# Attention and a gated feed-forward on one core: the weights' 64-bit words moved by four bytes in SBUF, and the output products' place in the order

## The chip, the cores and the metric

The kernel runs on one core of a Trainium2 chip. The metric is the device time of one execution, in microseconds. The engines are PE (TensorE, matrix products), DVE (VectorE), ACT (ScalarE), POOL (GpSimd) and SP (SyncE, which here issues every transfer). They run side by side, each its own instructions in the order in which the program has them; between engines they wait for semaphores.

## The reference

Attention over a window of 64 positions, 8 batches of 576 positions, 8 heads of 64, and behind it a feed-forward over 4,608 tokens from 512 to 2,048 and back to 512, with a piecewise gate:

```python
scores = np.where((rel >= 0) & (rel < window), scale * (q @ k.T), -1e9)   # rel = query position - key position
attn = softmax(scores) @ v
...
h = x @ w_in                                  # x: attention's output, 4608 x 512
g = np.where(h >= 1, h, np.where(h <= -1, 0.0, (h + 1) ** 2 / 4))
out = (g @ w_out).astype(np.float32)
```

q, k and v are float32; w_in and w_out are float64, and the kernel takes them as 64-bit words.

## The kernel before

**Tiles and steps.** The tokens are cut into twelve tiles (TILES): four of 256, six of 512, two of 256. Each tile runs the feed-forward in 16 steps f, one for each 128 of the 2,048 hidden channels. A step has two products on PE: the input product (`ffn_in`, L498), 12 matmuls into a PSUM bank `ps_h`, and the output product (`ffn_out`, L544), three matmuls for each 128 tokens, which add to the banks `acc`. Between them lies a chain over four engines: `ffn_relu` (L506, ACT), `ffn_square` (L512 on ACT, L514 on DVE), `ffn_gate` (L520, DVE, which also frees `ps_h`), `ffn_high` (L527, ACT, rounds the gate's result to `gh`) and `ffn_low` (L534, POOL, the rest `gl`). Each of `ps_h`, `a`, `gh` and `gl` has two buffers. The products take every operand as a high and a low part, so that three matmuls do the work of one exact one.

**Attention** goes in 36 blocks s of 128 tokens, ahead of the tile that needs them: scores on PE (L333), mask and maximum on DVE (L344, L348), exponentials on ACT (L355), inverse and normalization (L362, L363 and L367, DVE, now and then POOL), the transposition (L377, twelve instructions for each half of the heads on DVE, in two runs of six; in the first tiles on PE, L383, with a copy), the product with v (L397), and the result as a high part `xh` (a cast, L200 on ACT or L202 on DVE) and a low part `xl` (L413, DVE).

**Weights.** Each step needs a group of 64-bit words from w_in and w_out, 512 or 1,024 words a partition. They are loaded once (`w_load`, L218), in twenty transfers, into tiles of 16-bit numbers, `raw`. A 64-bit word is four such numbers, the lowest first. `w_rest` (L251, ACT) reads the two middle ones as one 32-bit integer (fraction) into `u`; `w_sign` (L228, ACT) reads the top one (sign and exponent) as bfloat16 and writes it into the front of the same tile; two limits (L232) and a shift (L244) on DVE bring the exponent to float32's place; `w_join` (L255, DVE) adds it to `u`; `w_high` (L202 or L200) casts `u` to the high part and `w_low` (L267, DVE) subtracts that from `u`. High and low part, `wts`, take the place of the raw words in SBUF. `u` has two buffers, so the third group's `w_rest` waits for the first one's `w_low`. The first four steps have two groups of 512 words each, the others one of 1,024.

[...] 

**The order** is the planner's (`Plan.run`). Each task has a key, and among the tasks that can start at about the same time on an engine (within PATIENCE; 0 on PE) the one with the lowest key is next. It reckons with costs in ns that are written in the code, and only the order comes out of it. An input product's key is `f * n / 384` past its tile's start, so in a 512 tile a step is 4/3 of a unit, in a 256 tile 2/3; the first two tiles run interleaved, 4/3 a step. The output product has the key of its input product plus `O_LAG`:

```python
x_out = add(
    key + O_LAG, dict(PE=3 * n / P * 232), lambda e, f=f: ffn_out(t, f),
    [xl, w_ready[f, 1]] + ([x_out] if f else []), ...
```

In the program as built, the twenty tiles of weights lie one behind the other at the end of SBUF, and each begins at a multiple of 32 bytes.

Of the kernel before, what the change touches and what calls it, by code (L numbers as in the profile page):

```python
# [12 lines left out]
U32 = mybir.dt.uint32  # L13
U16 = mybir.dt.uint16
# [6 lines left out]
P = 128  # L21
# [25 lines left out]
A_STEP = 4  # L47
A_SPAN = 8
A_LEAD = 5
O_LAG = 2.7  # L50
DMA_LAG = 2300
BEGIN = dict(PE=1500, ACT=2300, DVE=2500, SP=750)
PERIOD = 10240 / 3
# [11 lines left out]
class Plan:  # L65
# [9 lines left out]
    def add(self, key, cost, do, after=(), takes=(), gives=(), lag=0):  # L75
        self.work.append((key, cost, do, set(after), takes, gives, lag))
        return len(self.work) - 1
# [70 lines left out]
def banded_attention_then_ffn(ctx: ExitStack, tc: tile.TileContext, q, k, v, w, masks, out, dims):  # L148
    nc = tc.nc
# [30 lines left out]
    wpool = ctx.enter_context(tc.tile_pool(name="wpool", bufs=1))  # L180
# [25 lines left out]

    ws, wts, zs, us = {}, {}, {}, {}

    lowest, highest = 896 << 4, (1151 << 4) - 1

    def w_load(g):
        f, units = g
        m = len(units) * DM
        ws[g] = t = wpool.tile([P, 4 * m + 4], U16, name="raw", tag=f"w{f}_{units[0]}")
        src = w[f, :, units[0]:units[-1] + 1].bitcast(U16)
        nc.sync.dma_start(out=t[:, 1:4 * m + 1], in_=src.rearrange("p u n -> p (u n)"))  # L218

    def w_sign(g):  # L220

        m = len(g[1]) * DM
        t = ws[g].bitcast(BF16)
        zs[g] = z = t[:, :m]
        top = t[:, 4:4 * m + 4].rearrange("p (n h) -> p n h", h=4)[:, :, 0]
        nc.scalar.activation(z, top, AF.Prelu, scale=2.0 ** -48, alpha=2.0 ** -32)  # L228

    def w_limit(g, dt, lo, hi):  # L230
# [15 lines left out]
    def w_rest(g):  # L246

        m = len(g[1]) * DM
        us[g] = u = ffn.tile([P, 2 * DM], U32, name="u", bufs=BUFS["u"])[:, :m]
        rest = ws[g][:, 2:4 * m + 2].bitcast(U32).rearrange("p (n h) -> p n h", h=2)[:, :, 0]  # L250
        nc.scalar.activation(u, rest, AF.Copy, scale=2.0 ** -13)  # L251

    def w_join(g):
# [17 lines left out]
    def add_weights(f, units):  # L271
        g = f, units
        m = len(units) * DM
        act, dve1, dve2, dve4 = 93 + .833 * m, 68 + 1.0417 * m, 68 + .5208 * m, 68 + .2604 * m
        key = f * W_STEP - (W_FIRST[f] if f < len(W_FIRST) else W_LEAD) + .5 * units[0]
        x = add(W0_KEY + W0_STEP * (f + .5 * units[0]), dict(SP=W_LOAD * len(units)), lambda e: w_load(g), lag=DMA_LAG)
        xr = add(key - W_LATE, dict(ACT=act), lambda e: w_rest(g), [x], takes=["u"])
        x = add(key, dict(ACT=act), lambda e: w_sign(g), [xr])
        x = add(key, dict(DVE=dve4), lambda e: w_limit_signed(g), [x])
        x = add(key - W_LATE, dict(DVE=dve4), lambda e: w_limit_unsigned(g), [x])  # L280
        x = add(key - 2 * W_LATE, dict(DVE=dve4), lambda e: w_shift(g), [x])
        x = add(key - 3 * W_LATE, dict(DVE=dve1), lambda e: w_join(g), [x])
        x = add(key - 4 * W_LATE, dict(ACT=act, DVE=dve2), lambda e: w_high(g, e), [x])
        x = add(key - 5 * W_LATE, dict(DVE=dve1), lambda e: w_low(g), [x], gives=[("u", xr)])
        for u in units:
            w_ready[f, u] = x
# [250 lines left out]
    def ffn_out(t, f):  # L537
        _, gh, gl = gs.pop((t, f))
        if f == 0:
            acc[t] = [bank("acc") for _ in range(TILES[t] // P)]  # L540
        for i in range(TILES[t] // P):
            sub = slice(i * P, (i + 1) * P)
            for j, (g, part) in enumerate(((gh, 0), (gh, 1), (gl, 0))):
                nc.tensor.matmul(  # L544
                    acc[t][i], lhsT=g[:, sub], rhs=wts[f, 1][:, part], start=(f == 0 and j == 0),
                    stop=(f == NF - 1 and j == 2),
                )
# [16 lines left out]
    def add_ffn(t):  # L564
        n = TILES[t]
        x_out = None
        for f in range(NF):
# [14 lines left out]
            x_out = add(  # L582
                key + O_LAG, dict(PE=3 * n / P * 232), lambda e, f=f: ffn_out(t, f),
                [xl, w_ready[f, 1]] + ([x_out] if f else []), takes=["acc"] * (n // P) if f == 0 else [],
# [83 lines left out]
```

## Time and profile before

| | before |
|---|---|
| time, median of three runs | 944.24 us (942.72 to 944.29) |
| the profiled execution, its own time | 944.14 us |
| its span, first to last instruction | 942.4 us |
| PE busy | 916.6 us (97%) |
| DVE busy | 609.6 us (65%) |
| ACT busy | 462.7 us (49%) |
| POOL busy | 215.9 us (23%) |
| mean granted clock of PE | 0.994 |
| read from HBM, written | 59.44 MB, 9.44 MB |

The span is shorter than the execution's time by 1.7 us, which lie before its first and behind its last instruction. Busy time is a mean over stages that differ: the page has the span in 40 slices of 23.6 us, and there DVE is at nine tenths or more in the second to fifth, while PE is at nine tenths or more nearly throughout from the third on. The transfer engines are at eight tenths or more in the first two slices, at seven in the third, and at one or two tenths for most of the rest. A line that begins with a number is a timeline's (start in us, length in us, engine, line, operation, tiles written and read, count; in brackets how long the engine had been idle and what it waited for). In groups the columns behind the count are busy us and mean ns.

### The profile page before, as it was taken

The page shows a single profiled execution, that of the slowest core. Times are in us where ns is not written, and L with a number is a line of the kernel's source. Part 1 is how long each engine was busy: PE and PEld are TensorE (multiplying, and loading weights), DVE is VectorE, ACT ScalarE, POOL GpSimd, SP SyncE. Part 2 cuts the span into 40 slices and gives each one's busy share as a digit, 9 for nine tenths or more (in the row PEclk, how much of TensorE's full clock was granted, in tenths as well). Part 3 has the DMA queues.
Part 4 walks back from the last instruction along what each step waited for, and adds up shares of the span by engine and source line. Part 5 has one row for each costly group of instructions (what it writes and reads, how often), then busy time and mean ns, then how long its engine had stood idle before and what let it go on. Part 6 is the DMA issues. An engine that isn't in the chain of part 4 may idle for free.

```text
span 942.4 us, 16930 instructions
## 1 busy us (share of the span) xinstructions
PE 916.6 (97%) x6408; PEld 753.2 (80%) x6408; DVE 609.6 (65%) x1457; ACT 462.7 (49%) x1247; POOL 215.9 (23%) x204
## 2 busy tenths in 40 slices
PE   6798899999999999999999999999999999999998
PEld 5677788888887787777877777778777878888897
DVE  5999999897926755577466836683667561348511
ACT  5776766455534435444444434453445343436443
POOL 0132322222222212122212212122221222222222
PEclk8999999999999999999999999999999999999999
DMA  8971022222110212111211121211112020111000
GB/s 304 411 298 29 29 74 97 64 91 72 51 46 29 71 54 73 51 51 61 86 51 51 51 88 34 72 56 56 62 40 86 28 73 1 51 45 35 1 23 23
DMA packets 29025, 69.96 MB, mean 74 GB/s; under 512 B 3216, under 2 KB 3344, under 8 KB 27408
## 3 DMA queue, kind: packets, MB, share of 16 engines
q1 hardware_dynamic: 28944, 68.89, 21.4%
q8 instruction: 50, 0.82, 0.4%
q14 instruction: 31, 0.25, 0.1%
HBM read 59.44 MB, written 9.44 MB: 73 GB/s over the span
## 4 chain that ended last, share of the span: by engine, by line
PE 87%; DVE 7%; issue 3%; ACT 1%; POOL 1%; DMA 1%; SPq 0%; DVEq 0%; POOLq 0%; ACTq 0%
PE ps_h L498 40%; PE acc L544 40%; PE ps_a L397 4%; PE ps_a L333 3%; DVE u L255 2%; DVE raw L232 1%; DVE a L520 1%; DVE wts L202 1%; POOL gl L534 1%; DMA kt<-in_k 1%; DVE sm L367 1%; DVE raw L244 0%; DVE xl L413 0%; PE acc L397 0%; DVE wts L267 0%
## 5 line engine op out<-in xcount | busy, mean ns | idle before, releaser
L498 PE MATMUL ps_h<-xh,wts 128*128 128x256 f32 (+1 forms) x1536 | 408.8, 341 | 12.0 <-DVE a L520 8.9
L534 POOL TENSOR_TENSOR gl<-a,gh 128x256 fp32r<-128x256 f32 (+1 forms) x192 | 209.0, 1090 | 681.8 <-ACT gh L527 673.1
L544 PE MATMUL acc<-wts,gh 128*128 128x512 f32 x1152 | 364.9, 398 | 0.0
L498 PEld LDWEIGHTS ps_h<-xh,wts 128*128 128x128 f32 x1536 | 267.3, 188 | 57.0 <-DVE a L520 14.1
L498 PE MATMUL ps_h<-xl,wts 128*128 128x256 f32 (+1 forms) x768 | 259.3, 338 | 0.3 <-DVE xl L413 0.3
L544 PEld LDWEIGHTS acc<-wts,gh 128*128 128x128 f32 x1152 | 210.6, 188 | 46.4 <-issue 2.1
L520 DVE SCALAR_TENSOR_TENSOR a<-a,ps_h 128x256 f32<-128x256 f32 (+1 forms) x192 | 105.2, 553 | 215.3 <-ACT a L512 188.0
L544 PE MATMUL acc<-wts,gl 128*128 128x512 f32 x576 | 227.8, 395 | 0.1
L377 DVE STREAM_TRANSPOSE ptd<-sm 32x128 f32<-32x128 f32 x720 | 218.0, 303 | 12.4 <-POOL sm L367 0.9
L506 ACT ACTIVATE a<-ps_h 128x256 f32<-128x256 f32 (+1 forms) x192 | 93.6, 488 | 229.6 <-PE ps_h L498 219.4
L527 ACT CAST gh<-a 128x256 fp32r<-128x256 f32 (+1 forms) x192 | 97.5, 510 | 144.2 <-PE acc L544 120.0
L498 PEld LDWEIGHTS ps_h<-xl,wts 128*128 128x128 f32 x768 | 144.6, 188 | 18.4 <-DVE xl L413 0.5
L544 PEld LDWEIGHTS acc<-wts,gl 128*128 128x128 f32 x576 | 108.4, 188 | 26.8 <-POOL gl L534 1.1
L355 ACT ACTIVATE sm<-sm,nm 128x128 f32<-128x128 f32 x256 | 99.5, 390 | 52.9 <-DVE nm L348 52.9
L512 ACT ACTIVATE a<-a 128x512 f32<-128x512 f32 (+1 forms) x189 | 99.6, 527 | 5.9
L344 DVE SCALAR_TENSOR_TENSOR sm<-ps_a,msk 128x512 f32<-128x512 f32 x64 | 43.8, 684 | 13.2 <-PE ps_a L333 12.9
L413 DVE TENSOR_TENSOR xl<-ps_a,xh 128x512 fp32r<-128x512 f32 x34 | 23.5, 690 | 41.7 <-ACT xh L200 41.2
L367 DVE TENSOR_TENSOR sm<-sm,den 128x512 f32<-128x512 f32 x66 | 48.8, 739 | 2.3
L355 ACT ACTIVATION_READ_ACCUMULATOR sm<-sm,nm 128x1 f32 x256 | 47.9, 187 | 0.0
L348 DVE TENSOR_REDUCE nm<-sm 128x4 f32<-128x512 f32 x64 | 43.9, 686 | 2.1
L397 PEld LDWEIGHTS ps_a<-ptd,vt 128*64 128x64 f32 x1088 | 34.6, 138 | 12.7 <-PE acc L544 6.6
L333 PEld LDWEIGHTS ps_a<-kt,qt 64*64 64x64 f32 x1088 | 29.5, 132 | 13.3 <-issue 8.6
(54 smaller groups left out, 356.2 us busy)
## 6 DMA issues: line engine op xcount, KB each, us to landing
vt<-in_v SPq DMA_DIRECT2D x72, 256.0 KB, 2.9
kt<-in_k SPq DMA_DIRECT2D x36, 384.0 KB, 3.9
raw<-in_w SPq DMA_DIRECT2D x12, 1024.0 KB, 13.2
qt<-in_q SPq DMA_DIRECT2D x36, 256.0 KB, 2.7
out<-o SPq DMA_DIRECT2D x36, 256.0 KB, 2.0
raw<-in_w SPq DMA_DIRECT2D x8, 512.0 KB, 7.1
msk<-in_masks SPq DMA_DIRECT2D x1, 192.0 KB, 2.5
```

Source lines behind the costliest of these rows:

```text
L333: nc.tensor.matmul(banks[h][half[i], p, :], lhsT=qt[half[h], p, i * QB:(i + 1) * QB], rhs=kt[half[h], p, i * QB:i * QB + WIN], start=not m ...
L355: nc.scalar.activation(sm[:, p, :], (ps if masked else sm)[:, p, :], AF.Exp, bias=nm[:, p:p + 1], scale=scale if masked else 1.0, accum_ou ...
L367: engine[eng].tensor_tensor(out=sm, in0=sm, in1=den.unsqueeze(2).broadcast_to([P, NP, WIN]), op=ALU.mult)
L377: nc.vector.transpose(pt[c * SQ:(c + 1) * SQ, :, r], sm[r, :, c * SQ:(c + 1) * SQ])
L397: nc.tensor.matmul(ps[half[h], p, n], lhsT=vt[i][:, c:c + D], rhs=pt[h][:, p, n], start=True, stop=True)
L498: nc.tensor.matmul(ps[:, :n], lhsT=wts[f, 0][:, part, c * P:(c + 1) * P], rhs=x[:, c, :n], start=(c == 0 and j == 0), stop=(c == NP - 1 an ...
L506: nc.scalar.activation(gs[t, f][0][:, :n], phs[t, f][:, :n], AF.Relu, bias=0.5, scale=0.5)
L512: nc.scalar.activation(a[:, :n], a[:, :n], AF.Square)
L520: nc.vector.scalar_tensor_tensor(out=a[:, :n], in0=a[:, :n], scalar=1.0, in1=ps[:, :n], op0=ALU.min, op1=ALU.max)
L527: nc.scalar.copy(gh[:, :n], gs[t, f][0][:, :n])
L534: nc.gpsimd.tensor_tensor(out=gl[:, :n], in0=a[:, :n], in1=gh[:, :n].bitcast(F32), op=ALU.subtract)
L544: nc.tensor.matmul(acc[t][i], lhsT=g[:, sub], rhs=wts[f, 1][:, part], start=(f == 0 and j == 0), stop=(f == NF - 1 and j == 2),)
```

## The change

Two things. The load now drops the first 16-bit number of each partition's row and puts the rest at the tile's very start, so the middle numbers of a word begin at byte 0 and the top one at byte 4; the tile has no spare numbers, and a group takes 4,096 or 8,192 bytes a partition. (The dropped number is the lowest one of a row's first word, which nothing reads, as with the lowest ones of all other words.) And `O_LAG` goes from 2.7 to 2.5.

```diff
-O_LAG = 2.7
+O_LAG = 2.5
...
-        ws[g] = t = wpool.tile([P, 4 * m + 4], U16, name="raw", tag=f"w{f}_{units[0]}")
+        ws[g] = t = wpool.tile([P, 4 * m], U16, name="raw", tag=f"w{f}_{units[0]}")
         src = w[f, :, units[0]:units[-1] + 1].bitcast(U16)
-        nc.sync.dma_start(out=t[:, 1:4 * m + 1], in_=src.rearrange("p u n -> p (u n)"))
+        nc.sync.dma_start(out=t[:, :4 * m - 1], in_=src.rearrange("p u n -> p (u n)")[:, 1:])
...
-        top = t[:, 4:4 * m + 4].rearrange("p (n h) -> p n h", h=4)[:, :, 0]
+        top = t.rearrange("p (n h) -> p n h", h=4)[:, :, 2]
...
-        rest = ws[g][:, 2:4 * m + 2].bitcast(U32).rearrange("p (n h) -> p n h", h=2)[:, :, 0]
+        rest = ws[g].bitcast(U32).rearrange("p (n h) -> p n h", h=2)[:, :, 0]
```

A blank line was added too, so in the changed kernel every line behind L206 has a number higher by one (L544 is L545).

The layout alone changes no engine's order. O_LAG does. In a 512 tile, 2.7 lies just behind the key of the input product two steps on (2 x 4/3 = 2.67), 2.5 just ahead of it. The same holds for the first two tiles; in the other 256 tiles (2/3 a step) it is the input product four steps on. The order is the same up to about the eighth of the output products, some 53 us into the span; three places behind that follow.

PE in tile 6, where the input product of step 5 ends (`wts_816` is step 5's weights of the input side and of the output side, `wts_757` step 4's, `wts_699` step 3's; the numbers of the tiles in the other names don't matter). Before:

```order
L498 MATMUL ps_h_5217<-xl_4381,wts_816 128x512
L498 MATMUL ps_h_5217<-xh_4380,wts_816 128x512
L544 MATMUL acc_5117<-wts_699,gh_5188 128x512 x2
L544 MATMUL acc_5117<-wts_699,gl_5190 128x512
L544 MATMUL acc_5118<-wts_699,gh_5188 128x512 x2
```

and now:

```order
L499 MATMUL ps_h_5226<-xl_4408,wts_816 128x512
L499 MATMUL ps_h_5226<-xh_4407,wts_816 128x512
L545 MATMUL acc_5069<-wts_757,gh_5239 128x512 x2
L545 MATMUL acc_5069<-wts_757,gl_5241 128x512
L545 MATMUL acc_5070<-wts_757,gh_5239 128x512 x2
```

The output product behind step 5's input product was step 3's and is now step 4's.

ACT in the stage that prepares the weights, at about 60 us, from the relu and square of tile 1, step 3, to step 6's `w_sign` (L228; `raw_485` is step 6's group). L527 is the cast to `gh` of step 3, its first row tile 0, its second tile 1. Before:

```order
L506 ACTIVATE a_759<-ps_h_730 128x256
L512 ACTIVATE a_759<-a_759 128x256
L251 ACTIVATE u_770<-raw_485 128x1024
L527 CAST gh_789<-a_745 128x256
L527 CAST gh_792<-a_759 128x256
L228 ACTIVATE raw_485<-raw_485 128x1024
```

and now:

```order
L507 ACTIVATE a_766<-ps_h_744 128x256
L513 ACTIVATE a_766<-a_766 128x256
L528 CAST gh_771<-a_738 128x256
L528 CAST gh_791<-a_766 128x256
L252 ACTIVATE u_794<-raw_485 128x1024
L507 ACTIVATE a_813<-ps_h_775 128x256
L513 ACTIVATE a_813<-a_813 128x256
L229 ACTIVATE raw_485<-raw_485 128x1024
```

Both casts to `gh` now stand ahead of step 6's `w_rest`, and the relu and square of tile 0, step 4, ahead of its `w_sign`.

DVE from the last but one group's shift (L244) to the last group's limits (L232). Before:

```order
L244 TENSOR_SCALAR raw_826<-raw_826 128x1024
L255 TENSOR_TENSOR u_1266<-u_1266,raw_826 128x1024
L202 CAST wts_1546<-u_1266 128x2x512
L267 TENSOR_TENSOR wts_1546<-u_1266,wts_1546 128x2x512
L520 SCALAR_TENSOR_TENSOR a_1529<-a_1529,ps_h_1446 128x256
L232 TENSOR_SCALAR raw_864<-raw_864 128x1024
L413 TENSOR_TENSOR xl_1510<-ps_a_1550,xh_1509 128x4x128
```

and now:

```order
L245 TENSOR_SCALAR raw_825<-raw_825 128x1024
L256 TENSOR_TENSOR u_1270<-u_1270,raw_825 128x1024
L202 CAST wts_1565<-u_1270 128x2x512
L268 TENSOR_TENSOR wts_1565<-u_1270,wts_1565 128x2x512
L363 TENSOR_SCALAR den_1327<-den_1327 128x4
L364 RECIPROCAL den_1327<-den_1327 128x4
L368 TENSOR_TENSOR sm_1325<-sm_1325,den_1327 128x512
L521 SCALAR_TENSOR_TENSOR a_1511<-a_1511,ps_h_1457 128x256
L521 SCALAR_TENSOR_TENSOR a_1578<-a_1578,ps_h_1552 128x256
L233 TENSOR_SCALAR raw_863<-raw_863 128x1024 x2
```

An inverse and a normalization of block 5 now stand between the two, two gates stand together ahead of the last group's limits, and the xl subtraction is behind the last split.

## The prediction

> **What bounds the kernel now.** I began with the page: a span of 942.4 us and PE busy for 916.6 us of it, so some 26 us are to be had from waiting and the rest only from a faster pace of PE. Then I cut the span into stretches, to see where those 26 us lie.
>
> ```profile
> 0.00:53.00 53.00, 39.63 (x406) 31.62 (x407) 41.22 (x98) 36.28 (x112) 5.65 (x12) 0.90 0.96 365
> 53.00:137.30 84.30, 76.34 (x600) 64.69 (x598) 81.67 (x122) 58.10 (x129) 25.29 (x24) 1.00 0.24 85
> 137.30:938.20 800.90, 800.64 (x5405) 656.86 (x5404) 485.98 (x1239) 368.32 (x1008) 184.92 (x169) 1.00 0.17 54
> 938.20:942.40 4.20, 0.00 (x0) 0.00 (x0) 0.69 (x1) 0.00 (x0) 0.00 (x0) 0.92 0.34 127
> ```
>
> A row has the stretch and its length, then the busy time (and instructions) of PE, PEld, DVE, ACT and POOL, the granted clock, the DMA share and GB/s. Read the length against PE busy. Up to 53.0 us (filling) PE idles 13.4 us, from there to 137.3 us 8.0 us, then 0.3 us in 800.9, and 4.2 us at the end for the last store. So there are two machines. Until 137.3 us DVE sets the pace (81.7 of 84.3 us busy, and what the table doesn't count is the few tens of ns between instructions); afterwards it is PE alone. What hands over from one to the other stands in the timelines of DVE and PE:
>
> ```profile
> 133.96 1.37 DVE L255 TENSOR_TENSOR u<-u,raw 128x1024 uint16<-128x1024 uint16 x1
> 135.36 0.69 DVE L202 CAST wts<-u 128x1024 fp32r<-128x1024 f32 x1
> 136.09 1.23 DVE L267 TENSOR_TENSOR wts<-u,wts 128x1024 fp32r<-128x1024 f32 x1
> 137.23 0.41 DVE L520 SCALAR_TENSOR_TENSOR a<-a,ps_h 128x256 f32<-128x256 f32 x1
> ```
> ```profile
> 137.70 0.38 PE L498 MATMUL ps_h<-xh,wts 128*128 128x256 f32 x1 [0.26 <-DVE a L520]
> ```
>
> The last group of weights is split at 136.09, the gate of step 14 follows on DVE, and the product of tile 0, step 15 starts at once. From there PE never waits. **The time is therefore when DVE is through with that group and that gate, plus the PE work still to be done.**
>
> **The change part by part.** It has two: where the weights lie, and O_LAG, which only sets the order.
>
> *The layout.* No instruction is added or removed on PE, DVE, ACT or POOL; twenty loads carry 2 bytes less in each row. Could the old places have cost something? For the loads, set two stretches side by side, the first mostly weights (2 bytes off), the second only q, k, v and stores:
>
> ```profile
> 40.00:60.00 20.00, 18.69 (x137) 15.35 (x135) 19.21 (x35) 13.56 (x27) 4.27 (x5) 0.98 1.01 418
> 200.00:300.00 100.00, 100.00 (x735) 84.00 (x734) 64.96 (x167) 49.49 (x142) 23.53 (x25) 1.00 0.19 59
> ```
>
> 418 GB/s at a share of 1.01 against 59 at 0.19, which is 310 GB/s for full engines: the rows that start 2 bytes off move faster than the aligned shorter ones, so there is nothing to win. For the engines: the old tiles stand 4,128 or 8,224 bytes apart, so every other group starts 32 bytes off a multiple of 64. Step 15 above is such a group, step 4 is not; the split takes 1.23 us there and 1.22 here:
>
> ```profile
> 58.89 1.22 DVE L267 TENSOR_TENSOR wts<-u,wts 128x1024 fp32r<-128x1024 f32 x1
> 62.07 1.81 DVE L255 TENSOR_TENSOR u<-u,raw 128x1024 uint16<-128x1024 uint16 x1
> 63.91 1.07 DVE L202 CAST wts<-u 128x1024 fp32r<-128x1024 f32 x1
> ```
>
> I take 0 for the layout.
>
> *The order until 137 us.* Up to about 53 us the orders are the same. Behind that I count what DVE has in front of the last split, before and now. Gone are one copy of a transposed block (now ACT's) and one xl subtraction (now behind it); new are one cast to xh and one square, both ACT's before.
>
> ```profile
> L413 DVE TENSOR_TENSOR xl<-ps_a,xh 128x512 fp32r<-128x512 f32 x34 | 23.5, 690 | 41.7 <-ACT xh L200 41.2
> L202 DVE CAST xh<-ps_a 128x512 fp32r<-128x512 f32 x12 | 8.3, 689 | 6.7 <-PE ps_a L397 6.7
> L202 DVE COPY ptd<-ps_a 128x512 f32<-128x512 f32 x2 | 1.3, 680 | 0.0
> L514 DVE TENSOR_TENSOR a<-a 128x256 f32<-128x256 f32 x3 | 1.3, 418 | 0.0
> ```
>
> 689 + 418 - 680 - 690 = -263 ns. Second, the join (L255) and the cast (L202) are longer in some groups: 1.81 and 1.07 us at 62.07 and 63.91, against 1.37 and 0.69 at 133.96 and 135.36. POOL says why: at 62 us two subtractions run, at 134 us none.
>
> ```profile
> 61.66 2.77 POOL L534 TENSOR_TENSOR gl<-a,gh 128x256 fp32r<-128x256 f32 x2 [5.25 <-ACT gh L527]
> ```
> ```profile
> L255 DVE TENSOR_TENSOR u<-u,raw 128x1024 uint16<-128x1024 uint16 x12 | 20.0, 1668 | 0.4
> L202 DVE CAST wts<-u 128x1024 fp32r<-128x1024 f32 x12 | 9.8, 821 | 0.4
> ```
>
> Over the twelve large groups that costs 20.0 - 12 x 1.37 = 3.6 us and 9.8 - 12 x 0.69 = 1.5 us. [...]
>
> When POOL subtracts hangs on ACT's cast to gh. The new order moves it at several groups; at the one of 62 us both casts now stand in front of the next L251 instead of behind it, so the second subtraction ends before the cast at 63.91: -0.38 us. For the other groups the order tells no direction. The bounds are -5.1 us (none disturbed) and, with 1.81 and 1.07 in all twelve, 12 x 1.81 - 20.0 + 12 x 1.07 - 9.8 = +4.8 us. I take -0.4, near today's state, since most groups keep their ACT order.
>
> In front of the product at 137.70 PE now has one output product of a small tile more, and one attention product and one transposition less.
>
> ```profile
> 345.34 1.08 PE ps_a L397 x32
> 346.42 2.95 PE acc L544 x12
> 349.37 5.53 PE ps_h L498 x24
> 354.90 2.80 PE acc L544 x12
> 357.71 5.54 PE ps_h L498 x24
> 363.25 1.03 PE ps_a L333 x32
> 364.28 5.80 PE acc L544 x24
> 370.08 2.76 PE ps_h L498 x12
> ```
>
> These are pieces of the chain of waits (start, length, what; L498 is the input product, L544 the output product, L397 the attention product, L333 scores): a product of a 512 tile takes 2.8 us, of a 256 tile half, 1.4; an attention product 1.1; the transposition (four small matmuls) I put at 0.4. So 1.4 - 1.1 - 0.4 = -0.1 us is done earlier, and 0.1 us more is left afterwards.
>
> *The order after 137 us.* An output product used to run two steps behind its input product in the 512 tiles, now one. The pieces above show that the pace hardly depends on it: two input products in a row take 5.53, two output products 5.80, one of each 2.76 + 2.80 = 5.56. Per tile there are two more pairs of inputs and one more of outputs: 2 x (5.53 - 5.56) + (5.80 - 5.56) = +0.2, over six tiles 1.1 us, as one end. But the 5.80 begin behind scores, and an output product behind an attention product takes 2.95 instead of 2.80 by itself; without these 0.15 it is 0.0 a tile. I take 0. What the old lag gave was cover. One step's chain, from the relu to the subtraction, begins when the input product ends (469.29 + 2.76 = 472.05):
>
> ```profile
> 469.29 2.76 PE ps_h L498 x12
> ```
> ```profile
> 472.15 0.60 ACT L506 ACTIVATE a<-ps_h 128x512 f32<-128x512 f32 x1 [1.96 <-PE ps_h L498]
> 472.78 0.63 ACT L512 ACTIVATE a<-a 128x512 f32<-128x512 f32 x1
> 473.51 0.69 DVE L520 SCALAR_TENSOR_TENSOR a<-a,ps_h 128x512 f32<-128x512 f32 x1 [0.92 <-ACT a L512]
> 474.66 0.62 ACT L527 CAST gh<-a 128x512 fp32r<-128x512 f32 x1 [1.25 <-PE acc L544]
> 475.36 1.29 POOL L534 TENSOR_TENSOR gl<-a,gh 128x512 fp32r<-128x512 f32 x1 [3.80 <-ACT gh L527]
> ```
>
> It is over at 476.65, 4.6 us after the product. The tightest new place has one output and one input product between, 5.6 us: 1.0 us to spare. At the others a block of attention or another product stands between too. One place is short: in tile 9, DVE's order has the gate of step 14, the inverse (two such as the first row below, 0.4 us) and the normalization (0.7 us), all twelve transpositions (3.8 us), and only then the gate of step 15.
>
> ```profile
> 474.12 0.16 DVE L362 TENSOR_SCALAR den<-den 128x4 f32<-128x4 f32 x1
> ...
> 474.53 0.69 DVE L367 TENSOR_TENSOR sm<-sm,den 128x512 f32<-128x512 f32 x1
> 475.25 3.81 DVE L377 STREAM_TRANSPOSE ptd<-sm 32x128 f32<-32x128 f32 x12
> ```
>
> Step 14's gate ends 2.1 us after its product; 2.1 + 1.1 + 3.8 + 0.7 for the gate, + 0.7 for gh and + 1.4 for gl make 9.8 us, against 2.8 + 2.8 + 2.9 + 1.1 = 9.6 us of PE work in front of the output product. With a hand-over of 0.1 PE stalls +0.3 us. In the tiles before, six transpositions stand ahead of that gate and it is 1.6 us early.
>
> **Sum**, from the profiled execution (944.14 us: the span 942.4 and 1.7 around it; 0.1 below the median of 944.24): -0.3 - 0.4 + 0.1 + 0.3 = -0.3, so **943.9 us**.
>
> **The rivals.**
> (A) *POOL comes off the joins.* The alternation of input and output products spreads POOL's subtractions, and half of the 5.1 us go: 944.1 - 2.6 = 941.5 us. For it: two subtractions in a row (2.77 us) are what hits join and cast together. Against it: L251 still waits for DVE's split once a group, and ACT's casts to gh stay tied to it.
> (B) *The lag was cover, and PE waits in the 512 tiles.* At the tightest step, if the gate comes behind a full run of six transpositions (1.9 us), the chain needs 6.5 us where 5.6 are: 0.9 us in each of the five tiles (4 to 8) that carry attention, 4.5 us, 948.4 us. It begins once the gate waits over 1.0 us. For it: DVE's new order has six transpositions right in front of that gate. Against: they end, by their rows, about when ACT has the square ready.
> (C) *The loads slow down*, since each row's source now starts 2 bytes off and has an odd number of 16-bit words; this is the case in which the change isn't neutral to the transfers. Two groups of 512 KB are queued ahead of the second kt, for which PE waits at the start:
>
> ```profile
> PE acc L333 <- DMA kt<-in_k: 2.6, 1, 2.6
> ```
>
> At 418 GB/s they take 1.25 us each, and twice that would give 944.1 + 2.5 = 946.6 us. From 53 us on DVE is the bound and the loads are not: the rate there is down to 85 GB/s, so nearly all weights are in. [...]
> (D) *The aligned tiles are faster after all.* About half of DVE's 81.7 us until 137 us goes to groups of weights (join, cast and split of a large one alone take some 3.7 us), and 5% off that half would give 942.1 us. Against it the two splits of equal length above.
>
> **How the numbers follow.** Forecast 0.50, A 0.22, B 0.18, C 0.05, D 0.05. About 0.2% (1.9 us) is what a measurement of this kernel tells from no change. The forecast with its unknown of some 1.5 us either way lies within it; A and D fall below, B and C above: faster 0.27, same 0.50, slower 0.23. The range 940.0 to 948.6 takes in half of what POOL can give and more, and B's full price.
>
> **What would show it.** DVE's last split should start at 135.4 (136.09 now, less 0.7), the product of tile 0, step 15 at 137.0, and PE should have under 1 us of gaps behind it, the only one over 0.2 us in front of the last output product of tile 9. The mean of the joins should stay near 1,670 ns; 1,500 is A. Gaps of PE after each fifth input product, ended by POOL, are B; a raw load over 20 us to landing and a later second kt are C. I am wrong if the work of DVE up to the last split moves by over 2 us, or if PE idles in the 512 tiles.

## The result, and the profile after

| | before | changed |
|---|---|---|
| time, median | 944.0 us (942.72 to 944.29) | 934.11 us (933.44 to 934.33) |
| ratio, 95% interval | | 0.9897 (0.9879 to 0.9914) |
| the profiled execution, its own time | 944.14 us | 933.44 us |
| its span | 942.4 us | 931.7 us |
| PE busy | 916.6 us | 906.3 us |
| product of tile 0, step 15, starts at | 137.70 us | 137.25 us |

The change makes the kernel 1.0% faster, and the forecast was 943.9 us with a range from 940.0. The stretches of the changed kernel, cut where they were cut before (stretch, length, busy time of PE, PEld, DVE, ACT and POOL with the instructions, clock, DMA share, GB/s):

```profile
53.00:137.20 84.20, 74.56 (x563) 63.54 (x561) 81.61 (x121) 56.36 (x127) 26.23 (x24) 1.00 0.23 82
137.20:927.90 790.70, 790.64 (x5434) 658.36 (x5434) 487.31 (x1239) 371.92 (x1010) 177.41 (x165) 1.00 0.17 54
927.90:931.70 3.80, 0.03 (x1) 0.00 (x0) 0.69 (x1) 0.00 (x0) 0.00 (x0) 1.00 0.37 138
```

The stage of the weights is as long as it was. PE's own stretch has shrunk from 800.9 to 790.7 us, without a gap before or after: PE does no less work (5,405 matmuls before, 5,434 now) in 10 us less, and the granted clock was 1.00 in both stretches. So nothing was waited for less; the matmuls follow one another faster. The pieces of the chain of waits (start, length, what) in the changed kernel, where tile 5 begins:

```profile
350.47 8.16 PE ps_h L499 x36
358.63 5.44 PE acc L545 x24
364.07 2.72 PE ps_h L499 x12
366.79 1.03 PE ps_a L334 x32
367.82 2.99 PE acc L545 x12
370.81 2.72 PE ps_h L499 x12
373.53 2.72 PE acc L545 x12
```

A product of twelve matmuls takes 2.72 us whatever it is, 226.7 ns a matmul, except behind an attention product (scores, L334, or the product with v). The rows of before have 2.76, 2.80 and 5.53 (for two) at such places. In tiles 4 to 9 there are 192 products of 512 tokens; 0.05 us of each is about the 10 us.

The start times of single matmuls say the same in finer steps. In the changed kernel those inside a product are 227, 227, 226 ns apart, again and again (148 of the 192 products have no other distances, and the 44 others all stand behind an attention product); behind an attention product the distances are irregular (335, 231, 236, 228, 233, 230 ns after the product with v), six to eleven of them, and then settle. Before, most products never settled: 173 of the 192 have other distances among their last three.

### The profile page after: what moved, and what is told of

Its sections match the earlier page's. It is cut to its first block, busy times and chain, and to the rows that moved or that the text cites. A ratio compares the mean times of both kernels' runs of the same rounds, so it can differ in the third digit from the quotient of the medians.

```text
span 931.7 us, 16879 instructions
## 1 busy us (share of the span) xinstructions
PE 906.3 (97%) x6408; PEld 755.1 (81%) x6408; DVE 612.1 (66%) x1458; ACT 465.6 (50%) x1249; POOL 209.6 (22%) x201
## 4 chain that ended last, share of the span: by engine, by line
PE 87%; DVE 7%; issue 2%; ACT 2%; DMA 2%; POOL 1%; SPq 0%; DVEq 0%; ACTq 0%; POOLq 0%
PE acc L545 40%; PE ps_h L499 40%; PE ps_a L398 4%; PE ps_a L334 3%; DVE u L256 1%; DVE raw L233 1%; DVE a L521 1%; DMA vt<-in_v 1%; DVE wts L202 1%; DMA raw<-in_w 1%; POOL gl L535 1%; DVE wts L268 0%; DVE raw L245 0%; DVE sm L368 0%; ACT a L507 0%
## 5 line engine op out<-in xcount | busy, mean ns | idle before, releaser
L499 PE MATMUL ps_h<-xh,wts 128*128 128x256 f32 (+1 forms) x1536 | 406.3, 340 | 11.5 <-DVE a L521 10.5
L545 PE MATMUL acc<-wts,gh 128*128 128x512 f32 x1152 | 362.3, 396 | 0.0
L535 POOL TENSOR_TENSOR gl<-a,gh 128x256 fp32r<-128x256 f32 (+1 forms) x192 | 205.8, 1073 | 681.5 <-ACT gh L528 662.3
L499 PEld LDWEIGHTS ps_h<-xh,wts 128*128 128x128 f32 x1536 | 270.1, 190 | 53.4 <-DVE a L521 15.7
L545 PEld LDWEIGHTS acc<-wts,gh 128*128 128x128 f32 x1152 | 208.7, 188 | 42.2 <-issue 2.2
L545 PE MATMUL acc<-wts,gl 128*128 128x512 f32 x576 | 224.6, 390 | 0.0
L545 PEld LDWEIGHTS acc<-wts,gl 128*128 128x128 f32 x576 | 108.2, 188 | 24.4 <-POOL gl L535 0.7
L368 DVE TENSOR_TENSOR sm<-sm,den 128x512 f32<-128x512 f32 x69 | 52.0, 754 | 2.4
L398 PE MATMUL ps_a<-ptd,vt 128*64 128x64 f32 x1088 | 40.1, 227 | 1.9 <-DMA vt<-in_v 1.9
L334 PEld LDWEIGHTS ps_a<-kt,qt 64*64 64x64 f32 x1088 | 30.1, 135 | 11.9 <-issue 8.3
```

Of the source, the lines that this page charges most:

```text
L334: nc.tensor.matmul(banks[h][half[i], p, :], lhsT=qt[half[h], p, i * QB:(i + 1) * QB], rhs=kt[half[h], p, i * QB:i * QB + WIN], start=not m ...
L368: engine[eng].tensor_tensor(out=sm, in0=sm, in1=den.unsqueeze(2).broadcast_to([P, NP, WIN]), op=ALU.mult)
L398: nc.tensor.matmul(ps[half[h], p, n], lhsT=vt[i][:, c:c + D], rhs=pt[h][:, p, n], start=True, stop=True)
L499: nc.tensor.matmul(ps[:, :n], lhsT=wts[f, 0][:, part, c * P:(c + 1) * P], rhs=x[:, c, :n], start=(c == 0 and j == 0), stop=(c == NP - 1 an ...
L535: nc.gpsimd.tensor_tensor(out=gl[:, :n], in0=a[:, :n], in1=gh[:, :n].bitcast(F32), op=ALU.subtract)
L545: nc.tensor.matmul(acc[t][i], lhsT=g[:, sub], rhs=wts[f, 1][:, part], start=(f == 0 and j == 0), stop=(f == NF - 1 and j == 2),)
```

## The experiments

In the program as built the tiles of x start 128 bytes past a multiple of 256, gh and gl too, and every slice of them or of the weights that a matmul reads lies a multiple of 512 bytes further in. The first tile of weights also starts 128 past such a multiple. Before, each tile was 4,128 or 8,224 bytes behind the last, so each lay 32 bytes further on modulo 256, and of the twenty only the first, the ninth and the seventeenth agreed with x and gh: the input side of step 0, and steps 4 and 12. Now all do. The start times in tiles 4 to 9 of before fit this: the last four matmuls of a product are 226.7 ns apart in the input product of step 0 and the output products of 4 and 12 (the input products of these two, 229.7 and 228.8, are still settling in some tiles), and 232.7 to 235.0 in all products whose weights are an odd multiple of 32 bytes off. The remaining products, an even multiple off, have 228.1 to 233.4. Hence theory L: PE keeps 226.7 ns a matmul only where the operand that it loads and the one that it streams start at the same place modulo 256 bytes. (Agreement modulo 512 is not needed: in the changed kernel the weights lie an odd multiple of 256 bytes from x and a multiple of 512 from gh, and both kinds of product take 2.72 us.) All kernels below but the changed one itself have before's line numbers.

### The order alone, the layout alone, the pitch alone

```diff
-O_LAG = 2.7
+O_LAG = 2.5
```

That alone, on the kernel before:

> The layout of before with O_LAG 2.5. Theory L: the gain is the layout's, because PE's products keep the pace of 226.7 ns a 512-column matmul only where the operand it loads and the operand it streams start at the same place modulo 256 bytes; so the order alone gives what was forecast for it, 943 to 945 us, and the matmuls of the 512 tiles stay at about 234 ns. Rival O: the gain is the order's (alternating products run faster); then 934 to 935 us.

Measured: 944.0 us against 944.17, ratio 0.9997 (0.9987 to 1.0006). Its chain of waits in tile 5 has the old lengths:

```profile
361.55 5.58 PE acc L544 x24
367.13 2.76 PE ps_h L498 x12
...
376.68 2.80 PE acc L544 x12
379.48 2.79 PE ps_h L498 x12
```

O falls. The other half alone, the changed kernel with O_LAG back at 2.7:

> The layout of the changed kernel with O_LAG 2.7, so the order of before on every engine. Theory L: 933 to 936 us, most products of the 512 tiles at 2.72 us. Rival O: 943 to 945 us.

Measured: 932.65 us, ratio 0.9878 (0.9864 to 0.9893): all of the gain, and a little more than the whole change has. Its stretch of PE, and pieces of its chain:

```profile
136.30:926.10 789.80, 789.75 (x5404) 657.77 (x5404) 485.59 (x1237) 367.81 (x1008) 184.50 (x169) 1.00 0.17 54
```
```profile
360.88 5.71 PE acc L544 x24
366.59 2.72 PE ps_h L498 x12
369.31 2.72 PE acc L544 x12
```

Same order as before on every engine, the same 5,404 or 5,405 matmuls, 789.8 us instead of 800.9. Next, the loads and the place of the words left as before, and only the distance of the large tiles changed:

```diff
-        ws[g] = t = wpool.tile([P, 4 * m + 4], U16, name="raw", tag=f"w{f}_{units[0]}")
+        ws[g] = t = wpool.tile([P, 4 * m + (128 if m > DM else 4)], U16, name="raw", tag=f"w{f}_{units[0]}")
```

> Before with more spare numbers at the end of the twelve large tiles, so that each of them starts 128 bytes past a multiple of 256, as x, gh and gl do; the words stay two bytes in, the loads are those of before, the eight small tiles of steps 0 to 3 lie as before, O_LAG is 2.7. Theory L: steps 4 to 15 run as in the changed kernel and three quarters of the 10 us come: 936 to 938 us. Rival W: it is the place of the words in the tile or the load's shape that counts; then 943 to 945 us.

Measured: 936.44 us, ratio 0.9915 (0.9900 to 0.9930). W falls: no load and no read of the words was touched. Its chain shows both kinds of steps side by side:

```profile
366.68 2.75 PE ps_h L498 x12
369.43 2.81 PE acc L544 x12
...
374.97 2.80 PE acc L544 x12
...
388.54 2.72 PE acc L544 x12
391.26 2.72 PE ps_h L498 x12
```

The rows of 2.81 and 2.80 are the output products of steps 2 and 3, whose small tiles lie as before; those of 2.72 belong to steps 5 and 8. The 2.75 (step 4, agreeing) stands behind an output product that disagrees. In the kernel before the same product, also behind one that disagrees, has distances of 224 to 236 ns in tiles 5 to 9 and 226 and 227 only as its last two.

### Which places agree

The changed kernel with unused bytes ahead of some tiles, and nothing else. First 64 ahead of the weights:

```diff
     wpool = ctx.enter_context(tc.tile_pool(name="wpool", bufs=1))
+    wpool.tile([P, 32], U16, name="pad")
```

> The changed kernel with 64 unused bytes a partition ahead of the weights, so that all of them start 64 bytes further on against x, gh and gl. Theory L (the two operands must agree modulo 256): as in the steps of before with that offset, input products at about 233 ns a matmul, output products at about 229: 938 to 942 us. Rival A (it is enough that the weights start at a multiple of 64 bytes): 934 us, as the changed kernel.

Measured: 941.97 us, ratio 0.9976 (0.9965 to 0.9988). A falls: all weights start at multiples of 64 bytes, all equally far apart as in the changed kernel, and eight of the ten microseconds are gone. The input products take 2.80 us, the output products a little less:

```profile
377.15 2.79 PE acc L544 x12
379.94 2.80 PE ps_h L498 x12
382.74 2.76 PE acc L544 x12
385.50 2.80 PE ps_h L498 x12
```

In the tiles of 256 tokens it is the other way round. There an input product has matmuls of 256 columns, and with the operands 64 bytes apart it is the shorter one; first steps 10 and 7 of the last tile in the changed kernel, then in this run:

```profile
906.93 1.43 PE ps_h L499 x12
908.36 1.39 PE acc L545 x6
```
```profile
917.61 1.39 PE ps_h L498 x12
919.00 1.37 PE acc L544 x6
```

The single matmuls of these input products settle at 120 ns in the changed kernel and at 113 to 114 here. In these runs, then, what theory L says holds for matmuls of 512 columns only.

With 32 bytes (`[P, 16]`):

> The changed kernel with 32 unused bytes a partition ahead of the weights. Theory L (agreement of the two operands modulo 256): no product of a 512 tile comes down to 226.7 ns a matmul; by the odd steps of before 233 to 234 everywhere: 943 to 946 us. Rival A2 (what counts is that groups start at multiples of 4,096 bytes from one another): 934 us.

Measured: 946.45 us, ratio 1.0029 (1.0019 to 1.0038), half a microsecond above the range expected and slower than before. The regular layout, in which no group agrees, is the worse one:

```profile
376.83 2.80 PE acc L544 x12
379.63 2.80 PE ps_h L498 x12
382.43 2.80 PE acc L544 x12
```

The same 32 bytes, but ahead of everything, so that the weights lie where they lay in the last run and x, gh and gl move along:

```diff
+    const.tile([P, 16], U16, name="pad")
     idt = const.tile([P, P], F32, name="idt")
```

> The changed kernel with 32 unused bytes a partition ahead of everything, so that the weights lie where they lie in the run before, but x, gh and gl go along. Theory L: 934 us, as the changed kernel, since only the difference of the two places counts. Rival A (each operand has to start at a multiple of 64 bytes by itself): 943 to 946 us, as the run before.

Measured: 934.13 us, ratio 0.9895 (0.9880 to 0.9910), the time of the changed kernel. The weights have the addresses of the run before it and the pace of the changed kernel:

```profile
375.04 2.72 PE acc L544 x12
377.76 2.72 PE ps_h L498 x12
```

So for this pace no operand had to be aligned by itself; the two had to agree (934.13 us with all of them 32 bytes on, 946.45 with the weights alone). Then the two kinds of products were separated, with 64 bytes ahead of a, gh, gl and the weights, but behind x:

```diff
+    ffn.tile([P, 32], U16, name="pad", bufs=1)
     idt = const.tile([P, P], F32, name="idt")
```

> The changed kernel with 64 unused bytes a partition ahead of the tiles a, gh, gl and of the weights: weights against gh and gl agree, weights against x are 64 bytes apart. Theory L: output products at 226.7 ns as in the changed kernel, input products at 233; 96 input products of 512 tokens lose 0.065 us each, 934.1 + 6.2 = 940.3 us (939 to 942). Rival A: 934 us. Were it enough for one of the two kinds, both kinds would have one pace.

Measured: 939.65 us, ratio 0.9954 (0.9939 to 0.9968), where 940.3 was worked out:

```profile
375.57 2.74 PE acc L544 x12
378.32 2.80 PE ps_h L498 x12
381.11 2.74 PE acc L544 x12
383.86 2.80 PE ps_h L498 x12
```

Input products, whose two operands disagree, take 2.80 us; output products, whose operands agree, 2.74. The 0.02 above 2.72 are the settling behind each input product; the last four matmuls of an output product are 226.7 ns apart in most steps. Last, half of 256 (`[P, 64]` ahead of the weights):

> The changed kernel with 128 unused bytes a partition ahead of the weights: weights against x, gh and gl are half of 256 bytes apart. Theory L, with the pace of the steps of before with that distance (231 to 233 ns for the input products, 230 for the output products): 938 to 942 us. Rival A3 (a multiple of 128 bytes is enough): 934 us.

Measured: 946.46 us, ratio 1.0035 (1.0022 to 1.0048). A3 falls, and the expectation was missed by 4 us: the steps of before with this distance were too good a model.

```profile
376.60 2.78 PE acc L544 x12
379.38 2.78 PE ps_h L498 x12
...
395.81 2.80 PE acc L544 x12
```

The matmuls of this run alternate between 229 and 238 ns in many products and never come to 227.

### What O_LAG does in the new layout

The run of the layout alone was 1.5 us below the changed kernel, so both were run side by side. The change had already been run once more beside the kernels with shifted tiles:

> The changed kernel once more, beside the three others. All theories: 933.4 to 934.4 us.

> The new layout with O_LAG 2.7 once more, beside the changed kernel. Theory G (O_LAG 2.5 costs in the stage of the weights, as the last split 0.6 us later and the product of tile 0, step 15 1.7 us later than with 2.7, each counted from the tenth split and from the start, say): 932.5 us, 1 to 2 us below the changed kernel. Rival N (the difference of the two jobs is noise): within 0.5 us of it.

> The changed kernel beside the run with O_LAG 2.7. Theory G: 934.1 us, 1 to 2 us above it. Rival N: within 0.5 us of it.

The change again: three executions between 934.03 and 935.26 us, ratio 0.9899 (0.9882 to 0.9915); a fourth took 3,130.71 us, which is left out, and why is open. Side by side: 932.73 us (931.90 to 933.48) with 2.7, ratio 0.9889 (0.9873 to 0.9906); 933.69 us (933.40 to 935.33) with 2.5, ratio 0.9902 (0.9888 to 0.9917). The difference of 1.0 us is at the lower end of what G expected, and the intervals overlap; but the traces repeat it. From the start of the tenth split to the product of tile 0, step 15, it is 72.12 and 72.13 us in the two profiles with 2.7, and 73.31 and 73.34 with 2.5; behind that PE needs 789.79 and 789.81 against 790.67 and 790.69. The end of the stage in the changed kernel, on DVE and PE:

```profile
135.65 1.23 DVE L268 TENSOR_TENSOR wts<-u,wts 128x1024 fp32r<-128x1024 f32 x1
136.79 0.75 DVE L521 SCALAR_TENSOR_TENSOR a<-a,ps_h 128x256 f32<-128x256 f32 x2
```
```profile
137.25 0.39 PE L499 MATMUL ps_h<-xh,wts 128*128 128x256 f32 x1 [1.70 <-DVE a L521]
```

and with 2.7 in the new layout:

```profile
134.74 1.23 DVE L267 TENSOR_TENSOR wts<-u,wts 128x1024 fp32r<-128x1024 f32 x1
135.88 0.41 DVE L520 SCALAR_TENSOR_TENSOR a<-a,ps_h 128x256 f32<-128x256 f32 x1
```
```profile
136.35 0.39 PE L498 MATMUL ps_h<-xh,wts 128*128 128x256 f32 x1 [0.20 <-DVE a L520]
```

With 2.5 two gates stand behind the last split, but the product waits only for the first, which ends at 137.20. It starts 1.61 us behind the start of the last split in both, and PE idles longer in front of it (1.70 us instead of 0.20) because it is through with its other work earlier. The difference lies ahead of that: from the tenth split to the last it is 70.51 and 70.52 us with 2.7, 71.70 and 71.73 with 2.5. Of the 2.1 us that 2.5 costs in these two stretches, the pair run side by side shows 0.7 given back ahead of the tenth split and 0.4 behind PE's last matmul. Why PE needs 0.9 us more behind the product was not taken apart. The new layout with the old O_LAG is the best version found, about 1 us below the changed kernel.

## Why the prediction was wrong

**The step that failed** is "I take 0 for the layout". Its two reasons stand: the loads did not change their pace, and DVE's split takes the same 1.23 us. But it asked only who writes and converts the weights, in a stage of 137 us. It did not ask PE, which reads them in every product for 800 us. Measured, the layout by itself is worth -11.5 us (932.65 against 944.17; -10.5 when repeated), and 10.7 of them are PE's pace: 800.50 us from the product of tile 0, step 15 to PE's last matmul before, 789.79 with the layout alone. That PE alone set the time after 137 us was the prediction's first finding; an edit that moves PE's operands had to be weighed there first.

From start to start, PE's matmuls of 512 columns took 11.8 us less in that stretch and those of 256 columns 1.1 more. The two profiled executions are 12.0 us apart. Of the rest, 0.6 lie between the tenth split and the last (71.07 and 70.51), where a split and a subtraction of POOL start within 12 ns of each other: before, the split took 1.81 us and the subtraction 0.74, with the layout alone it is 1.23 and 1.81; 0.8 lie ahead of the tenth split, whose start varies from 63.2 to 65.5 us between the profiles, whatever the layout.

The two signs by which the prediction would have called itself wrong, over 2 us on DVE or idle time of PE, did not come; neither of them looks at PE's pace.

**The sign was in the rows.** The prediction took products of 2.76, 2.80 and 5.80 / 2 = 2.90 us for one pace with differences by kind and neighbour. In the 5.80 most is indeed the neighbour, the scores ahead of it: with the layout alone that place still has 5.71. The rest was a disturbed pace that changed with the step: the same kind of product took 2.75 us in one step and 2.80 in the next, and repeated that in every tile. A duration that depends on nothing but which tile is read can point to where that tile lies.

**The order's sum** of -0.3 us came out as -0.2 in the kernel before (944.0 against 944.17, no difference that can be told), but its terms were not right. In front of the last split, -0.7 us were forecast; from the tenth split to the last it was 71.07 us before and is 71.70 in the changed kernel and 71.67 with the order alone, so +0.6. The four exchanged instructions came out as forecast (-0.2 in that stretch with the order alone). What POOL disturbs did not: the joins there lost 0.9 us, but the casts gained 1.3 and the normalizations 0.4, where -0.4 in all had been taken. The groups of the changed kernel, over the whole span, show joins that got shorter and casts that got longer:

```profile
L256 DVE TENSOR_TENSOR u<-u,raw 128x1024 uint16<-128x1024 uint16 x12 | 18.7, 1556 | 0.4
L202 DVE CAST wts<-u 128x1024 fp32r<-128x1024 f32 x12 | 10.8, 901 | 0.4
```

Joins 1.3 us less, casts 1.0 more (20.0 and 9.8 before). Of the twelve joins eight took over 1.7 us before and five do now, and of the casts four took over 1.0 us and six do now. Each of these long ones, in both kernels, began while a subtraction of POOL ran, and none of the short ones did (joins of 1.36 to 1.39 us, casts of 0.69 to 0.70). So POOL's subtractions moved from one to the other and did not go. That is rival A's beginning and its end. Behind the handover the order alone left 800.09 us instead of 800.50, and 3.73 instead of 4.17 for the end, which pay for the stage; that the sum came out near is luck.

**The stall in tile 9** was forecast at 0.3 us in front of the last output product. POOL's last subtraction of the tile ends at 830.19, and the product's third matmul, which reads it, starts at 830.24:

```profile
828.91 1.28 POOL L535 TENSOR_TENSOR gl<-a,gh 128x512 fp32r<-128x512 f32 x1 [4.19 <-ACT gh L528]
```
```profile
830.24 0.50 PE L545 MATMUL acc<-wts,gl 128*128 128x512 f32 x1
```

It and the one behind it start 333 and 334 ns after their forerunners, where 231 and 236 are usual at that place: 0.2 us, at the forecast place, by the forecast cause.

**The rivals.** B did not happen: apart from that 0.2 us PE waits nowhere between 138 and 927 us, so one step was cover enough. C did not either; the loads of the changed kernel, 2 bytes into the rows and with an odd count (the last number is us to landing):

```profile
raw<-in_w SPq DMA_DIRECT2D x12, 1023.8 KB, 12.3
...
raw<-in_w SPq DMA_DIRECT2D x8, 511.8 KB, 7.4
```

Packets of 8,190 bytes took 309 ns (median), those of 8,192 before 313. D had the right edit and sign but looked at DVE.

**What stays open** is the mechanism. With the same instructions, 233.3 or 226.7 ns a matmul hang on how the two operands lie to each other, and no run here shows what in PE or SBUF makes it so, nor why it is 256 bytes that count. Why matmuls of 256 columns are faster with the operands 64 bytes apart than in agreement is open too.

## What to carry to other kernels

Where PE sets the time, compare the start-to-start distance of equal matmuls across tiles; if it depends on which tile is read, look at the start addresses of the loaded and the streamed operand. For float32r matmuls of 512 columns, make them agree modulo 256 bytes, by the length of the tiles or a pad ahead of a pool (here 226.7 ns a matmul instead of 228.1 to 235.0); for other widths, measure first. Spare bytes at the end of a tile are not free: they move every tile behind it (here 32 bytes further on with each tile, and PE needed 800.50 us instead of 789.79). And an edit that shifts buffers is to be priced first on the engine that sets the time, even if the edit's code belongs to another.

## What the hardware showed unexpectedly

- Twelve float32r matmuls of 512 columns, each with its own weights and not behind attention, take 2.72 us (226.7 ns each) if the two operands start at the same place modulo 256 bytes, and 2.76 to 2.81 us otherwise, with 32, 64 and 128 bytes between them in the runs above. Absolute alignment to 64 bytes was neither enough (941.97 us with all weights at such places) nor needed (934.13 us with everything 32 bytes off).
- At 64 bytes it matters which operand lies further on. With the loaded one ahead, the last matmuls of a product are 233.2 to 233.5 ns apart, in input products and in the output product of step 10 of the kernel before; with the streamed one ahead, the products of the kernel before end at 228.1 to 229.6.
- For matmuls of 256 columns agreement was not the best place: 120 ns each in the changed kernel, 113 to 114 with the loaded operand 64 bytes further on.
- The pace settles: after a run of small matmuls (attention), where the operands agree, the first two large ones start 335 to 341 ns apart and the next 224 to 240, six to eleven distances in all, before they come to 227.
